# Routed steps of retention plus mixture-of-depths: spread over slots, compared from PSUM, two routing banks

## The chip, the cores and the metric

The kernel runs on one core of one Trainium2 chip. A core has TensorE (PE, matrix products into PSUM), VectorE (DVE), ScalarE (ACT), GpSimd (POOL) and the DMA queues, here issued from SyncE (SP) and POOL. Each engine works its own instructions in the order in which the program issues them; between engines there are only semaphores. The metric is device microseconds of one launch; lower is better. The trace is of one profiled execution, and times in it count from the first instruction.

## The reference

Two stages. The first is a recurrent retention over 4 batches, 8 heads, 768 positions and head size 64; the second routes 128 of the 768 tokens of each batch through a small feed-forward network (FFN) and adds the result to them.

```python
# retention, per batch b and head h
state = gamma[h] * state + outer(k[t], v[t])
y[t] = q[t] @ state / sqrt(64)

# mixture of depths; x is y with the heads side by side, 512 wide
scores = x @ w_gate
top = the 128 tokens of each batch with the largest scores
h = relu(x[top] @ w1)              # 512 -> 1024
out = x
out[top] = x[top] + sigmoid(scores[top]) * (h @ w2)
```

## The kernel before

**Retention in chunks.** The decay is folded into q and v by two tables of powers, so that a chunk of 128 positions needs only a masked product of q and k, a product with the running state, and an update of that state. There are 6 chunks to a batch and 24 in all. They come two at a time: block `m` (12 of them) holds chunks 2m and 2m+1, and is loaded, cast and turned as a whole.

**The main loop** goes over the blocks. In block `m` it issues: `load(m + 5)` on SP's queue (3 loads of 512 KB); `cast(m + 3)` on POOL (L147 to L150: q times its table, k, v times its table, to bf16); and then, for each of the block's two chunks, `transposes(m + 2, "q")` or `(..., "k")` (eight PE transposes into `pt`, one ACT copy), `scores(m + 1, ...)` (16 matmuls into `pa`, then DVE multiplies by the mask, L180), `combine` (`py`: the state's part L193, the masked part L199), `update` (state product L214 into `pst`, two ACT copies L219), `finish` (L227: ACT copies `py` to `xo`; L229: DVE multiplies `py` by `w_gate` and sums each row to a gate score), and `put` (store of `xo` on SP's queue).

**Routing.** After a batch's sixth chunk, `routed(b)` gives a list of twelve steps. The main loop takes one step off the list at four places in each block, before `combine` and after `finish` of each chunk, so the list lasts three blocks; the last batch's list runs after the loop. The steps are:

- `route_rows` (two steps): PE spreads each chunk's 128 scores over all partitions (L249), ACT copies them to `row` (L251).
- `route_beats`: for each of 6 chunks DVE compares the scores pairwise, within the chunk (L260; `before` breaks ties) and against all later chunks (L262, which also counts).
- `route_ranks`: 21 PE matmuls with a column of ones count who beats each token (L271); DVE adds to `rank`, and six compares with `slot` (L280) give one-hot rows `P`.
- `route_index`: 12 matmuls turn `P` into token numbers; DVE casts them to `idx` (L293).
- `route_fetch`: POOL issues a gather of 128 rows of the output (L299). One step is empty after it.
- `route_turn` and `route_gate`: PE turns the rows, ACT copies them (`xT`); DVE multiplies by `w_gate` and sums (L319), ACT and DVE make the sigmoid.
- `ffn_up` twice (16 matmuls each, L335, and an ACT relu into `hT`), `ffn_down` (8 matmuls, L343, and DVE's scaled add into `ye`, L345), `route_put` (POOL issues the scatter, L350).

**Order and buffers.** The schedule is manual: instructions stand on each engine in the order of these calls. PSUM is split by pools: `psT` 2 banks for `pt`, `psA` the two-bank `pa`, `psY` 2 for `py`, `psS` 1 for `pst`, `psM` 1 for everything of the routing. Two engines that read the same PSUM tile are ordered by a semaphore: L229 waits for L227. Loads have 5 buffers each and `xo` has 4. Since SP's queue is in order, `load(m + 5)` stands behind the stores of block m - 1; on POOL the gather and the scatter stand between the casts.

Of the kernel before, what the change touches and what calls it, by code (L numbers as in the profile page):

```python
# [18 lines left out]
def kernel(ctx: ExitStack, tc: tile.TileContext, q, k, v, w_gate, w1, w2, capacity, out):  # L19
    nc = tc.nc  # L20
# [24 lines left out]
    psT = ctx.enter_context(tc.tile_pool(name="psT", bufs=2, space=bass.MemoryType.PSUM))  # L45
# [3 lines left out]
    psM = ctx.enter_context(tc.tile_pool(name="psM", bufs=1, space=bass.MemoryType.PSUM))  # L49
# [56 lines left out]
    slot = consts.tile([128, C], BF)  # L106
    before = consts.tile([128, C], FT)
    tok = consts.tile([128, 1 + NBC], BF)
    above = consts.tile([128, NC], FT)

    def route_tables():
        slot_i = consts.tile([128, C], I32)
        nc.gpsimd.iota(slot_i, pattern=[[1, C]], base=0, channel_multiplier=0)
        nc.vector.tensor_copy(slot, slot_i)
        nc.gpsimd.memset(before, TINY)
# [6 lines left out]
        above_i = consts.tile([128, NC], I32)  # L122
        nc.gpsimd.iota(above_i, pattern=[[-C, NC]], base=C * (NC - 1), channel_multiplier=0)
        nc.vector.tensor_copy(above, above_i)
# [115 lines left out]
    def route_rows(b, lo):  # L240
        st = batch[b]
        if lo == 0:
            st["row"] = perb.tile([128, S], FT, name="row", tag="row")
            st["beats"] = perb.tile([128, NC, S], BF, name="beats", tag="beats")
            st["lost"] = perb.tile([128, NC], FT, name="lost", tag="lost")
        n = min(4, NC - lo)
        pr = psM.tile([128, n * C], FT, name="pr", tag="pm")
        for j in range(n):
            nc.tensor.transpose(pr[:, j * C:(j + 1) * C],  # L249
                                st["sc"][:, lo + j:lo + j + 1].to_broadcast([128, C]), identf)  # L250
        nc.scalar.activation(st["row"][:, lo * C:(lo + n) * C], pr, AF.Copy)  # L251


    def route_beats(b, blocks):
        st = batch[b]
        row, g = st["row"], st["beats"]
        for I in blocks:
            s = st["sc"][:, I:I + 1]
            lo, hi = I * C, (I + 1) * C
            nc.vector.scalar_tensor_tensor(g[:, I, lo:hi], row[:, lo:hi], s, before, OP.subtract, OP.is_lt)  # L260
            if hi < S:
                nc.vector.tensor_scalar(g[:, I, hi:], row[:, hi:], s, None, OP.is_le, OP.add,  # L262
                                        accum_out=st["lost"][:, I:I + 1])

    def route_ranks(b):
        st = batch[b]
        g = st["beats"]
        pk = psM.tile([128, 512], FT, name="pk", tag="pm")
        for J in range(NC):
            for I in range(J + 1):  # L270
                nc.tensor.matmul(pk[:, J:J + 1], g[:, I, J * C:(J + 1) * C], ones,  # L271
                                 start=(I == 0 and J == 0), stop=True, skip_group_check=True)
        won = perb.tile([128, NC], FT, name="won", tag="won")
        nc.vector.tensor_sub(won[:, :NC - 1], above[:, :NC - 1], st["lost"][:, :NC - 1])
        nc.vector.tensor_copy(won[:, NC - 1:], above[:, NC - 1:])
        rank = perb.tile([128, NC], FT, name="rank", tag="rank")
        nc.vector.tensor_add(rank, pk[:, :NC], won)
        P = perb.tile([128, NC, C], BF, name="P", tag="P")
        for J in range(NC):
            nc.vector.tensor_scalar(P[:, J, :], slot, rank[:, J:J + 1], None, OP.is_equal)  # L280
        st["P"] = P

    def route_index(b):
# [8 lines left out]
        idx = perb.tile([128, 1], I32, name="idx", tag="idx")  # L292
        nc.vector.tensor_copy(idx, pi[:, 0:1])  # L293
        st["idx"] = idx

    def route_fetch(b):
        st = batch[b]
        xg = perb.tile([128, Dm], FT, name="xg", tag="xg")
# [16 lines left out]
    def route_gate(b):  # L315
        st = batch[b]
        junk = store.tile([C, H, D], BF, name="junk", tag="junk")
        ssel = perb.tile([128, 1], FT, name="ssel", tag="ssel")
        nc.vector.scalar_tensor_tensor(junk.opt(), st["xg"], 1.0, wgB, OP.mult, OP.mult, accum_out=ssel)  # L319
# [19 lines left out]
    def ffn_down(b):  # L339
        st = batch[b]  # L340
        pd = psM.tile([128, Dm], FT, name="pd", tag="pm")
        for ff in range(FB):
            nc.tensor.matmul(pd, st["hT"][:, ff, :], w2s[:, ff, :], start=(ff == 0), stop=(ff == FB - 1))  # L343
        ye = perb.tile([128, Dm], FT, name="ye", tag="ye")
        nc.vector.scalar_tensor_tensor(ye, pd, st["gate"][:, 0:1], st["xg"], OP.mult, OP.add)  # L345
        st["ye"] = ye
# [7 lines left out]
    def routed(b):  # L354
        return [
            lambda: route_rows(b, 0),
            lambda: (route_rows(b, 4), route_beats(b, range(0, 2))),
            lambda: route_beats(b, range(2, NC)),
            lambda: route_ranks(b),
            lambda: route_index(b),  # L360
            lambda: route_fetch(b),
            lambda: None,
            lambda: (route_turn(b), route_gate(b)),
            lambda: ffn_up(b, 0),
            lambda: ffn_up(b, 1),
            lambda: ffn_down(b),
            lambda: route_put(b),
        ]


# [11 lines left out]
    pending = []  # L382

    def step():
        if pending:
# [67 lines left out]
```

## Time and profile before

| what | value |
|---|---|
| median of 3 runs | 178.52 us (177.93 to 178.78) |
| the profiled execution, its own time | 179.37 us |
| its span, first to last instruction | 177.5 us |
| mean granted TensorE clock | 0.831 |
| busy: PE, DVE, ACT, POOL | 119.0, 84.0, 69.9, 72.7 us |
| first attention product of block 0 | at 22.65 us |
| HBM read and written | 24.38 MB, 7.34 MB |

The page cuts the span in 40 slices of 4.44 us and gives each engine's busy share in tenths, the clock that TensorE was granted, and the share of the DMA engines. A group's line gives line number, engine, operation, output and inputs, shapes and count; then busy time and the mean of one in ns; then how long the engine sat idle just before them and what ended that. A line of the timeline gives start, duration, engine, source line, operation and, in brackets, the idle time before it and its releaser. A matmul row can merge several matmuls. Loads of weights into PE are counted apart (PEld) and lie beside the matmuls.

### The profile page before, as it was taken

The numbers are of one execution on the slowest core, as the hardware profiler recorded it, in microseconds if no ns is written. First come the engines' busy times: TensorE is split into PE (matmuls) and PEld (weight loads), VectorE is DVE, ScalarE is ACT, GpSimd is POOL, SyncE is SP. The second block draws the span as 40 slices with busy tenths as digits, with TensorE's granted clock in tenths as the row PEclk, the third lists the DMA queues.
The fourth block names the chain that finished last, engine by engine and source line by source line (L and its number), as shares of the span: only waits on it lengthen the run. The fifth ranks groups of instructions, "written<-read, shape, count | busy, mean of one in ns | idle before, by whom it ended". The sixth has DMA issues, their size and how long they took to land. (4 is left out here: it accounts for less than half of the span.)

```text
span 177.5 us, 3719 instructions
## 1 busy us (share of the span) xinstructions
PE 119.0 (67%) x1528; PEld 92.6 (52%) x1532; DVE 84.0 (47%) x204; ACT 69.9 (39%) x129; POOL 72.7 (41%) x64
## 2 busy tenths in 40 slices
PE   0325299658969279699931499999479798342860
PEld 0314178546758158586820388868258684132720
DVE  1032045343074993544589954655993512851010
ACT  8135076442365324456760036668503452201110
POOL 7898970268966906600796039002002001120002
PEclk9999999999999999999995555699855558955567
DMA  4999999999999999696495003113303201301001
GB/s 136 297 299 290 275 216 213 252 298 285 340 315 322 326 312 310 205 278 198 118 301 174 4 0 122 59 63 118 120 2 93 90 0 59 118 0 59 4 0 59
DMA packets 43265, 29.86 MB, mean 168 GB/s; under 512 B 1136, under 2 KB 39024, under 8 KB 43248
## 3 DMA queue, kind: packets, MB, share of 16 engines
q1 hardware_dynamic: 41040, 25.43, 51.7%
q0 software_dynamic: 2208, 4.19, 10.4%
q8 instruction: 12, 0.20, 0.4%
q14 instruction: 5, 0.04, 0.1%
HBM read 24.38 MB, written 7.34 MB: 179 GB/s over the span
## 5 line engine op out<-in xcount | busy, mean ns | idle before, releaser
L229 DVE SCALAR_TENSOR_TENSOR junk<-py,wgB 128x512 bf16<-128x512 f32 x24 | 16.5, 689 | 46.6 <-ACT xo L227 46.6
L180 DVE TENSOR_TENSOR am<-pa,causal 128x1024 bf16<-128x1024 f32 x24 | 29.3, 1219 | 12.5 <-PE pa L177 12.3
L162 ACT ACTIVATE qT<-pt 128x1024 bf16<-128x1024 bf16 x12 | 15.8, 1319 | 32.2 <-PE pt L159 32.2
L219 ACT ACTIVATE S<-pst 64x256 bf16<-64x256 f32 x40 | 15.1, 378 | 33.3 <-PE pst L214 32.8
L150 POOL TENSOR_TENSOR vb<-vf,gv 128x1024 bf16<-128x1024 f32 x12 | 22.8, 1900 | 6.1 <-DMA vf<-in_v_dram 6.1
L350 POOL DMA_INDIRECT out_dram<-ye,idx x4 | 4.1, 1037 | 50.4 <-DVE ye L345 38.9
L147 POOL TENSOR_TENSOR qb<-qf,gq 128x1024 bf16<-128x1024 f32 x12 | 22.8, 1904 | 2.6 <-DMA qf<-in_q_dram 2.3
L159 PE MATMUL pt<-ident,qb 128*128 128x128 bf16 x96 | 11.6, 296 | 17.6 <-POOL qb L147 17.6
L271 PE MATMUL pk<-ones,beats 128*128 128x1 bf16 x84 | 8.9, 175 | 18.9 <-DVE beats L260 11.5
L199 PE MATMUL py<-vb,am 64*128 64x64 bf16 x384 | 21.5, 222 | 0.0
L199 PEld LDWEIGHTS <-am 64*128 64x128 bf16 x384 | 18.1, 115 | 4.2 <-issue 3.6
L159 PEld LDWEIGHTS <-qb 128*128 128x128 bf16 x96 | 9.0, 136 | 18.8 <-POOL qb L147 18.3
L299 POOL DMA_INDIRECT xg<-out_dram,idx x4 | 4.3, 1074 | 34.3 <-DVE idx L293 34.3
L227 ACT ACTIVATE xo<-py 128x512 f32<-128x512 f32 x24 | 14.3, 597 | 9.9 <-PE py L199 7.1
L214 PE MATMUL pst<-vb,kb 64*128 64x128 bf16 x160 | 18.2, 281 | 0.0
L271 PEld LDWEIGHTS <-beats 128*128 128x128 bf16 x84 | 5.5, 105 | 22.7 <-DVE beats L260 15.0
L260 DVE SCALAR_TENSOR_TENSOR beats<-row,sc,before 128x128 bf16<-128x128 f32 x24 | 17.0, 710 | 0.0
L177 PE MATMUL pa<-qT,kT 64*64 64x128 bf16 x384 | 14.1, 289 | 3.0 <-DVE am L180 1.7
L149 POOL CAST kb<-kf 128x1024 bf16<-128x1024 f32 x12 | 12.5, 1042 | 7.2 <-DMA kf<-in_k_dram 7.2
L335 PE MATMUL ph<-xT,w1s 128*128 128x128 bf16 x128 | 13.4, 289 | 2.4 <-ACT xT L311 1.7
L214 PEld LDWEIGHTS <-kb 64*128 64x128 bf16 x160 | 14.3, 128 | 0.0
L335 PEld LDWEIGHTS <-w1s 128*128 128x128 bf16 x128 | 11.9, 135 | 3.8 <-issue 3.6
(62 smaller groups left out, 151.9 us busy)
## 6 DMA issues: line engine op xcount, KB each, us to landing
qf<-in_q_dram SPq DMA_DIRECT2D x12, 512.0 KB, 6.3
kf<-in_k_dram SPq DMA_DIRECT2D x12, 512.0 KB, 7.4
vf<-in_v_dram SPq DMA_DIRECT2D x12, 512.0 KB, 7.6
out_dram<-xo SPq DMA_DIRECT2D x24, 256.0 KB, 3.8
w1s<-in_moe_w_dram POOLq DMA_DIRECT2D x1, 1024.0 KB, 10.9
w2s<-in_moe_w_dram POOLq DMA_DIRECT2D x1, 1024.0 KB, 17.2
wgB<-in_moe_w_gate_dram SPq DMA_DIRECT2D x1, 256.0 KB, 6.3
xg<-out_dram,idx POOLq DMA_INDIRECT x4, 3.4
```

The costliest lines, as they stand in the source:

```text
L147: nc.gpsimd.tensor_mul(qb, raw["q", m].rearrange("p h j d -> p j h d"), gq[:, 2 * r:2 * r + 2, :, None].to_broadcast([128, 2, H, D]))
L150: nc.gpsimd.tensor_mul(vb, raw["v", m].rearrange("p h j d -> p j h d"), gv[:, 2 * r:2 * r + 2, :, None].to_broadcast([128, 2, H, D]))
L159: nc.tensor.transpose(pt[:, j, dd, :], src[:, j, 2 * dd:2 * dd + 2, :], ident)
L162: nc.scalar.activation(t.rearrange("p h (s j) -> p j h s", j=2), pt, AF.Copy)
L180: nc.vector.tensor_mul(am.rearrange("p a b c d -> p (a b c d)"), pa.rearrange("p a b c d -> p (a b c d)"), causal.rearrange("p a b c -> p ...
L199: nc.tensor.matmul(py[:, h, :], att[m, dd // 2][r, half, dd % 2, j, :], vb[r, j, h, :], start=(c == 0 and h == 0 and j == 0), stop=True, s ...
L214: nc.tensor.matmul(pstate[b][:, dd, :], kb[r, j, 2 * dd:2 * dd + 2, :], vb[r, j, 2 * dd:2 * dd + 2, :], start=(c == 0 and dd == 0 and j == ...
L219: nc.scalar.activation(t[r, :, half * 64:half * 64 + 64], pstate[b][r, :, half * 64:half * 64 + 64], AF.Copy)
L229: nc.vector.scalar_tensor_tensor(junk.opt(), py.opt(), 1.0, wgB, OP.mult, OP.mult, accum_out=batch[b]["sc"][:, c:c + 1])
L260: nc.vector.scalar_tensor_tensor(g[:, I, lo:hi], row[:, lo:hi], s, before, OP.subtract, OP.is_lt)
L271: nc.tensor.matmul(pk[:, J:J + 1], g[:, I, J * C:(J + 1) * C], ones, start=(I == 0 and J == 0), stop=True, skip_group_check=True)
L335: nc.tensor.matmul(ph[:, j, :], w1s[:, dd, ff * 128:(ff + 1) * 128], st["xT"][:, dd, :], start=(j == 0 and dd == 0), stop=True, skip_group ...
```

## The change

**Slots.** The list of steps is replaced by a table of slots. Chunk i begins at slot t = 2i; slot t is worked between `scores` and `combine`, slot t + 1 between `finish` and `put`; what is left after the loop is worked in order. `route_spread` of a chunk is at t + 3 and `route_beats` at t + 4, so that each chunk of a batch is compared while later ones are still being computed, with the earlier chunks of its batch in place of the later ones. After a batch's last chunk follow ranks (t + 5), hot rows (t + 6), index (t + 7), fetch (t + 8), turn and gate (t + 11), sigmoid and the first `ffn_up` (t + 12), the second (t + 13), `ffn_down` (t + 14), `ffn_add` (t + 15), put (t + 16). For batch 2 the slots t + 12 and t + 13 fall in chunk 23, the rest after the loop.

**Engines and operands.** The comparison within the chunk reads the spread scores `pr` in PSUM; ACT's copy of `pr` to `row` is issued behind it (the program gives it a semaphore wait on that comparison). The counts of the first five chunks are made by `route_part`, after the fifth, so that `route_ranks` has six matmuls left, and one that spreads the slot numbers over the partitions of PSUM. One compare of 768 columns makes `P`, with the slot numbers read from PSUM. The gate product moves from DVE to a POOL multiply (L335 of the new file) and an ACT copy with a sum (L337). Several steps are cut where they change engine, so that the DVE part falls in a later slot than the PE part.

**Banks.** `psT` has one bank in place of two, `psM` two in place of one.

```diff
-    psT = ctx.enter_context(tc.tile_pool(name="psT", bufs=2, space=bass.MemoryType.PSUM))
+    psT = ctx.enter_context(tc.tile_pool(name="psT", bufs=1, space=bass.MemoryType.PSUM))
...
-    psM = ctx.enter_context(tc.tile_pool(name="psM", bufs=1, space=bass.MemoryType.PSUM))
+    psM = ctx.enter_context(tc.tile_pool(name="psM", bufs=2, space=bass.MemoryType.PSUM))
...
-    slot = consts.tile([128, C], BF)
+    slot = consts.tile([1, C], BF)
+    one = consts.tile([1, C], BF)
...
-    above = consts.tile([128, NC], FT)
+    won = consts.tile([128, NC], FT)
...
+    def route_spread(b, c):
+        st = batch[b]
+        if c == 0:
+            st["row"] = perb.tile([128, S - C], FT, name="row", tag="row")
             st["beats"] = perb.tile([128, NC, S], BF, name="beats", tag="beats")
+            st["part"] = perb.tile([128, NC], FT, name="part", tag="part")
+        pr = psM.tile([128, C], FT, name="pr", tag="pm")
+        nc.tensor.transpose(pr, st["sc"][:, c:c + 1].to_broadcast([128, C]), identf)
+        st["pr"] = pr
+
+    def route_beats(b, c):
+        st = batch[b]
+        row, g, pr = st["row"], st["beats"], st["pr"]
+        lo, hi = c * C, (c + 1) * C
+        s = st["sc"][:, c:c + 1]
+        nc.vector.scalar_tensor_tensor(g[:, c, lo:hi], pr, s, before, OP.subtract, OP.is_lt)
+        if c < NC - 1:
+            nc.scalar.activation(row[:, lo:hi], pr, AF.Copy)
+        if c:
+            acc = won[:, c:c + 1] if c < NC - 1 else st["part"][:, c:c + 1]
+            nc.vector.tensor_scalar(g[:, c, :lo], row[:, :lo], s, float(lo), OP.is_lt, OP.subtract, accum_out=acc)
+
+    def route_part(b):
...
         pk = psM.tile([128, 512], FT, name="pk", tag="pm")
+        for J in range(NC - 1):
+            for c in range(J, NC - 1):
+                nc.tensor.matmul(pk[:, J:J + 1], g[:, c, J * C:(J + 1) * C], ones,
+                                 start=(J == 0 and c == 0), stop=True, skip_group_check=True)
+        st["pk0"] = pk
+
+    def route_part_add(b):
+        st = batch[b]
+        nc.vector.tensor_add(st["part"][:, :NC - 1], st["pk0"][:, :NC - 1], won[:, :NC - 1])
+
+    def route_ranks(b):
...
+        nc.tensor.matmul(pk[:, C:2 * C], one, slot, start=True, stop=True, skip_group_check=True)
         for J in range(NC):
...
+            nc.tensor.matmul(pk[:, J:J + 1], g[:, NC - 1, J * C:(J + 1) * C], ones,
+                             start=False, stop=True, skip_group_check=True)
+        st["pk"] = pk
+
+    def route_hot(b):
...
+        nc.vector.tensor_add(rank, pk[:, :NC], st["part"])
         P = perb.tile([128, NC, C], BF, name="P", tag="P")
-        for J in range(NC):
-            nc.vector.tensor_scalar(P[:, J, :], slot, rank[:, J:J + 1], None, OP.is_equal)
+        nc.vector.tensor_tensor(P, pk[:, None, C:2 * C].to_broadcast([128, NC, C]),
+                                rank[:, :, None].to_broadcast([128, NC, C]), OP.is_equal)
...
     def route_gate(b):
         st = batch[b]
-        junk = store.tile([C, H, D], BF, name="junk", tag="junk")
+        prod = perb.tile([128, Dm], FT, name="prod", tag="prod")
+        nc.gpsimd.tensor_mul(prod, st["xg"], wgB)
         ssel = perb.tile([128, 1], FT, name="ssel", tag="ssel")
-        nc.vector.scalar_tensor_tensor(junk.opt(), st["xg"], 1.0, wgB, OP.mult, OP.mult, accum_out=ssel)
+        nc.scalar.activation(prod, prod, AF.Copy, accum_out=ssel)
...
+    for i in range(NBC):
+        b, c = divmod(i, NC)
+        t = 2 * i
+        at(t + 3, route_spread, b, c)
+        at(t + 4, route_beats, b, c)
+        if c == NC - 2:
+            at(t + 5, route_part, b)
+            at(t + 6, route_part_add, b)
+        if c == NC - 1:
+            for d, f in ((5, route_ranks), (6, route_hot), (7, route_index), (8, route_fetch), (11, route_turn),
+                         (11, route_gate), (12, route_sigmoid)):
+                at(t + d, f, b)
+            at(t + 12, ffn_up, b, 0)
+            at(t + 13, ffn_up, b, 1)
+            at(t + 14, ffn_down, b)
+            at(t + 15, ffn_add, b)
+            at(t + 16, route_put, b)
...
+        for u, nm in enumerate(("q", "k")):
+            t = 2 * (2 * m + u)
+            if m + 2 < NBLK:
+                transposes(m + 2, nm)
+            if m + 1 < NBLK:
+                scores(m + 1, u)
+            slot_work(t)
+            py = combine(m, u)
+            update(m, u)
+            xo = finish(m, u, py)
+            slot_work(t + 1)
+            put(m, u, xo)
+    for t in sorted(slots):
+        slot_work(t)
```

## The prediction

> **What bounds the kernel now.** I read the page first, then the groups with their shapes, the timeline around the longest waits, the stretches with the clock, and the end of the timeline. The chain of waits breaks off at the last gather, so the timeline had to carry the rest.
>
> The page (slices of 4.44 us):
>
> ```profile
> span 177.5 us, 3719 instructions
> PE 119.0 (67%) x1528; PEld 92.6 (52%) x1532; DVE 84.0 (47%) x204; ACT 69.9 (39%) x129; POOL 72.7 (41%) x64
> ...
> PE   0325299658969279699931499999479798342860
> ...
> POOL 7898970268966906600796039002002001120002
> PEclk9999999999999999999995555699855558955567
> DMA  4999999999999999696495003113303201301001
> ```
>
> No engine is full over the span. DMA is full for about 72 us, then nearly idle; PE is full in most slices after that, with holes near 60, 93, 127 and 155 us. Until about 50 us PE waits for data. Two groups (columns: busy us, mean ns; idle before):
>
> ```profile
> L271 PE MATMUL pk<-ones,beats 128*128 128x1 bf16 x84 | 8.9, 175 | 18.9 <-DVE beats L260 11.5 <-DVE beats L262 5.0 <-ACT row L251 0.5
> L260 DVE SCALAR_TENSOR_TENSOR beats<-row,sc,before 128x128 bf16<-128x128 f32 x24 | 17.0, 710 | 0.0
> ```
>
> PE idles 18.9 us ahead of the rank counts. The comparison has a median of 344 ns but a mean of 710: three of the 24 took 1.94, 1.56 and 6.33 us. The timeline shows what lay beside the longest:
>
> ```profile
> 89.48 1.89 POOL L150 TENSOR_TENSOR vb<-vf,gv 128x1024 bf16<-128x1024 f32 x1
> ...
> 89.89 6.33 DVE L260 SCALAR_TENSOR_TENSOR beats<-row,sc,before 128x128 bf16<-128x128 f32 x1
> ...
> 94.18 1.89 POOL L150 TENSOR_TENSOR vb<-vf,gv 128x1024 bf16<-128x1024 f32 x1
> 96.14 0.87 DVE L262 TENSOR_SCALAR_CACHE_REDUCE beats<-row,sc 128x640 bf16<-128x640 f32 x1
> ...
> 96.28 0.18 PE L271 MATMUL pk<-ones,beats 128*128 128x1 bf16 x1 [6.03 <-DVE beats L260]
> ```
>
> The comparison starts under a POOL multiply and ends when POOL's unbroken run of five ends (94.18 + 1.89 = 96.07). The other two also end with a POOL multiply. Comparisons with two SBUF tensors (`row`, `before`) are held; the counting form (L262, one tensor) never was. Excess: 17.0 - 24 x 0.344 = 8.7 us. The holes also cost clock (columns of interest: PE busy, then after POOL the granted clock):
>
> ```profile
> 84.00:88.00 4.00, 4.00 (x78) 3.17 (x76) 2.59 (x4) 2.48 (x4) 2.44 (x2) 1.00 0.29 98
> 104.00:108.00 4.00, 4.00 (x55) 3.14 (x53) 1.13 (x3) 1.87 (x4) 3.06 (x3) 0.50 0.22 66
> 120.00:124.00 4.00, 4.00 (x86) 3.21 (x82) 1.93 (x4) 3.57 (x7) 1.04 (x1) 1.00 0.35 131
> ```
>
> At 0.50 the eight transposes of a half block take 1.04 us, at 1.00 0.61. (Before about 79 us the column says 1.00 while they take 1.04; I read that stretch as slow.) The clock rises near 79, 113 and 148 us, each time during `ffn_up` or `ffn_down`, and falls after each hole.
>
> The end:
>
> ```profile
> 149.49 0.64 PE L199 MATMUL py<-vb,am 64*128 64x64 bf16 x16
> ...
> 158.75 1.03 POOL L299 DMA_INDIRECT xg<-out_dram,idx  x1 [7.33 <-DVE idx L293]
> ...
> 173.51 1.01 POOL L350 DMA_INDIRECT out_dram<-ye,idx  x1 [13.72 <-DVE ye L345]
> ```
>
> The last attention product (I count 24 chunks, 0 to 23) ends at 150.1; 8.65 us later the last gather is issued, and 18.75 us after that the span ends. The profiled execution took 179.37 us, 1.87 over its span and 0.85 over the median 178.52.
>
> **The change part by part.**
>
> *To chunk 6's state copy* (54.1 us before): data-bound. The added spreads and comparisons hide under that. One PSUM bank for turned q and k makes each turn wait for the previous copy (1.3 us), but turns are 4 us apart. I take 54.4.
>
> *Comparisons.* All 24 now take `pr` from PSUM, so one SBUF tensor. The 8.7 us go and 24 x 0.344 stays. Could PSUM be dearer? L229 reads `py` from PSUM in 691 ns; L319, the same operation on SBUF, takes 689: nothing. The Trainium skill ("Perfetto Trace Analysis", Optimizing Scalar/DVE Operations) gives DVE about 60 ns of overhead on SBUF and 125 on PSUM; by it 24 x 65 ns = 1.6 us more. The row is the same shape on this chip, so I keep nothing.
>
> *A new wait.* `row`'s copy on ACT now waits for the comparison that reads the same bank, as L229 waits for L227's copy of `py` today (46.6 us of DVE waiting). Behind it on ACT stand the state copy and `xo`. This closes a ring: state copy 0.80, `xo` 0.63, gate score 0.62, mask product 1.14 (1.22 less overlap), comparison 0.40, `row` 0.25 (128x256 takes 0.379, 128x512 0.588, so 0.27), next state copy. That is 3.85 us a chunk, in which PE has about 2.4 us of attention at the high clock (87.94 to 90.2: 2.3, plus one spread 0.15) and 4.2 at the low one (24.47 to 28.36: 3.9, plus 0.26). So attention is PE-bound at the low clock and ring-bound at the high one.
>
> *Chunks 6 to 12, low clock.* Six chunks x 4.2 = 25.2. Batch 0's routed work on the way: seven rank matmuls 0.8 (13 in 1.5), hot rows on DVE 1.1, index 0.64, turn 0.9, two halves of `ffn_up` 1.7 and 1.4, `ffn_down` 1.8: 8.3. Less 1.5 for state products that chunks 11 and 12 don't have. 54.4 + 32.0 = 86.4, against 87.8 before.
>
> *Chunks 12 to 23.* Nothing now holds DVE for 6 us, and PE has work in every chunk, so I expect the clock up from `ffn_up` (about 80) on. Eleven rings x 3.85 = 42.4. Extra per batch: `ye` 0.75 and, as a spread needs the bank that `ye` frees, turn and scores behind it 1.1; hot rows 1.15 (six compares take 1.07; the 768-wide form scaled from L180 0.91, at most 1.22); `idx` and gate 0.5; the FFN's ACT copies 1.5: 5.0, twice. Less 2 for the last four chunks, which have no turns and then no scores. 50.4. The last product stands 1.8 ahead of that point: 86.4 + 48.6 = 135.0. At the low clock throughout, PE needs 11 x (4.2 + 1.8 of routed work) = 66, and the product ends at about 150.6. I take three quarters high: 135.0 + 0.25 x 15.6 = 138.9.
>
> *Gate product.* Moved from DVE (0.69) to POOL: 1.90/2 = 0.95, at most 1.9, plus an ACT sum near 0.6 (`xo` 0.597). POOL's queue puts the casts of one block (4.85) between gather and product, ACT waits up to 1.5 us once a batch (inside my 5.0). At the end it runs beside turn, copy and `ffn_up`: `e` is due 2.8 us after the rows land, the first `hT` at 3.8, so nothing.
>
> *The end.* Batch 2's second `ffn_up` and `ffn_down` move behind chunk 23's product, ahead of the last spread. From the product: `ffn_up` 1.0, `hT` 0.75, `ffn_down` 1.8, fifteen counts 1.5 (they hide `ye`, the scatter's wait), spread 0.2, two compares 1.35, counts 0.8, hot rows 1.3, index 0.8, `idx` and issue 0.5: 10.0 instead of 8.65. Low clock throughout would make it 12.5. Gather to end stays 18.75.
>
> Sum: 138.9 + 10.0 + 18.75 = 167.7 of span, plus 1.87: 169.5 beside 179.37, which is 9.9 less; from the median, 168.6. I state 168.5.
>
> **The rivals.**
>
> 1. *PE stays at the low clock.* For: PE idles about a third of each ring, and the first 79 us show dense attention without a rise. Against: from 84 to 90 and 119 to 125 us attention alone held 1.00, and it fell only after holes of 2.5 to 4 us. Span 150.6 + 12 + 18.75 = 181.4, so 182.3 at the pessimistic end; with the first FFN stretch high, 174. Together: 173 to 182. The skill ("TensorE: Matmul & The Clock Gate", A second HAM failure mode: psum-queue depth-cycling) says frequent short PE idles between groups can make the clock oscillate, which speaks against one turning bank; the whole low clock is what it would make of the time at worst. The two stretches at 1.00 are dense ones, so no row here excludes it.
>
> 2. *The ring is longer than the sum of its rows* (the other side). Place: ACT's copy of `row` behind DVE, once a chunk. The span equals today's if the product ends at 148.75: (148.75 - 54.4)/17 = 5.55 us a chunk, against 4.97 in my sum. Another 0.6 a chunk, for example the counting comparison (0.33 to 0.87) falling inside, turns it to slower; 1 us more gives 186. For: six handovers, each across engines, on in-order queues. Against: the durations include today's handovers.
>
> 3. *The ring doesn't bind*: ACT is often late anyway and PE, all high, sets 3.45 a chunk: product at 127, time about 157.
>
> 4. *The stalls go but were slack.* Before, DVE's 6.3 us left PE idle for 6.03, so I give this little: 178.
>
> **How the numbers follow.** Forecast (160 to 173) 0.60; rival 1 0.16, of which 0.05 above 179.4; rival 2 0.12; rival 3 (below 160) 0.08; rival 4 0.04. Half a per cent is 0.9 us, about what three runs from 177.93 to 178.78 can tell. Faster: 0.60 + 0.10 + 0.08 = 0.78 with most of rival 1; same: 0.05; slower: 0.17. The range reaches into rivals 1 and 2 above and rival 3 below: 159 to 181.
>
> **What would show it.** All 24 comparisons near 0.35 us; DVE's wait on `xo` still long; a new ACT wait of `row` on the comparison of about 0.5 us, some twenty times; no PE hole over 3 us between 55 and 135 us; the clock at 1.00 from about 80 to the last gather; the last gather near 149. I am wrong if the clock column shows 0.50 for most of 90 to 135, if state copies stand over 5 us apart where no FFN runs, or if POOL multiplies still lengthen a DVE comparison.

## The result and the profile after

| | before | predicted | after |
|---|---|---|---|
| median, us | 178.65 (177.93 to 179.05, 4 runs) | 168.5 | 166.8 (165.17 to 168.52, 4 runs) |
| ratio to before, 95% interval | | | 0.9311 [0.9231, 0.939] |
| state copy of chunk 6 starts | 54.12 | 54.4 | 53.90 |
| state copy of chunk 12 starts | 87.84 | 86.4 | 84.91 |
| last attention product ends | 150.1 | 138.9 | 139.73 |
| last gather issued | 158.75 | 148.9 | 149.14 |
| span ends | 177.5 | 167.7 | 164.7 |

The kernel is 11.9 us faster. The ratio leaves out the run of 168.52, which is over 1.5% above the fastest of its kernel. The profiled execution took 166.44 us, 1.74 over its span. The page of the kernel after, in slices of 4.12 us:

```profile
span 164.7 us, 3709 instructions
PE 117.8 (72%) x1532; PEld 92.9 (56%) x1536; DVE 72.6 (44%) x173; ACT 74.9 (45%) x149; POOL 77.7 (47%) x67
...
PE   0234289984969799968976899999489868830770
...
POOL 7978993039895682588606706900200220022302
PEclk9999999999999999999998555569955555985589
```

The empty stretch of PE that stood near 93 us before is gone, and DVE is busy 72.6 us where it was busy 84.0. But the clock row is not the forecast one: from slice 23 (about 91 us) it says 5 more often than 9. Three groups (busy us, mean ns; idle before, and what ended it):

```profile
L258 DVE SCALAR_TENSOR_TENSOR beats<-pr,sc,before 128x128 bf16<-128x128 f32 x24 | 8.2, 342 | 0.5 <-PE pr L250 0.5
...
L260 ACT ACTIVATE row<-pr 128x128 f32<-128x128 f32 x20 | 5.5, 276 | 20.7 <-DVE beats L258 20.7
...
L250 PE MATMUL pr<-identf,sc 128*128 128x128 f32 x24 | 10.1, 421 | 7.0 <-DVE ye L372 5.4 <-DVE junk L229 1.4
```

The first: 24 comparisons cost 8.2 us of DVE, not 17.0, and the longest is 0.351. The second is the forecast wait of the row copy, twice as long as forecast. The third was not priced as a stop of PE: the spread needs a routing bank that `ye` (L372, the add that ends the FFN) still reads. The timeline of the kernel after shows the first such wait:

```profile
84.80 0.53 PE L271 MATMUL pk<-ones,beats 128*128 128x1 bf16 x15
...
86.34 0.69 DVE L229 SCALAR_TENSOR_TENSOR junk<-py,wgB 128x512 bf16<-128x512 f32 x1 [2.12 <-ACT xo L227]
...
86.95 0.75 DVE L372 SCALAR_TENSOR_TENSOR ye<-pd,gt,xg 128x512 f32<-128x512 f32 x1
...
87.76 0.32 PE L250 MATMUL pr<-identf,sc 128*128 128x128 f32 x1 [2.43 <-DVE ye L372]
```

The last matmul of `ye`'s input ends at 83.85, but `ye` stands on DVE behind the gate score of the next chunk, which waits for ACT's copy. PE stands for 2.43 us, again for 2.43 at 118.30, and for 0.49 in the tail. The stretches with the clock (length; busy and instructions of PE, PEld, DVE, ACT, POOL; clock; DMA share; GB/s):

```profile
84.00:88.00 4.00, 1.57 (x41) 1.37 (x38) 1.58 (x5) 1.35 (x3) 0.01 (x1) 1.00 1.16 310
...
100.00:104.00 4.00, 4.00 (x54) 3.18 (x52) 1.97 (x8) 2.84 (x5) 3.63 (x3) 0.50 0.36 117
...
116.00:120.00 4.00, 1.70 (x40) 1.39 (x41) 1.46 (x4) 1.72 (x3) 1.04 (x1) 1.00 0.17 66
```

Both waits fall where the clock is at 1.00, and it drops within 1.8 us of the end of each (89.4 and 120.1). The end of the span, after and then before:

```profile
138.70 1.03 PE L199 MATMUL py<-vb,am 64*128 64x64 bf16 x16
...
149.14 1.04 POOL L316 DMA_INDIRECT xg<-out_dram,idx  x1 [3.31 <-DVE idx L313]
...
154.39 3.47 PE L358 MATMUL ph<-xT,w1s 128*128 128x128 bf16 x32 [0.69 <-ACT xT L328]
...
157.70 1.89 PE L366 MATMUL pd<-w2s,hT 128*128 128x512 bf16 x7
...
160.66 1.04 POOL L377 DMA_INDIRECT out_dram<-ye,idx  x1 [6.77 <-DVE ye L372]
```

```profile
164.07 1.86 PE L335 MATMUL ph<-xT,w1s 128*128 128x128 bf16 x16 [0.68 <-ACT xT L311]
...
166.62 1.87 PE L335 MATMUL ph<-xT,w1s 128*128 128x128 bf16 x16 [0.68 <-ACT hT L337]
...
169.98 2.46 PE L343 MATMUL pd<-w2s,hT 128*128 128x512 bf16 x6 [0.22 <-issue]
```

With one routing bank the second half of `ffn_up` waited for the relu `hT` of the first, and `ffn_down` waited again and ran at the low clock. With two banks the halves run as one row, the clock rises at 157.6, and `ffn_down` takes 1.89; before it rose only at 172.0, near the end of `ffn_down`, which took 3.27 (169.17 to 172.44). From the start of `ffn_up` to the end of `ffn_down` it is 159.59 - 154.39 = 5.20 against 172.44 - 164.07 = 8.37 (169.98 + 2.46 ends at 172.44). Of the 3.17 us saved, 1.37 are the two waits of PE for `hT` (0.69 and 0.68); most of the rest is the clock. That the clock rises sooner because the row has no gaps is read from these rows. No run isolates it, but the same stretch takes 8.61 us in the first experiment below, which has one bank, and 3.67 to 5.61 in the other nine, which have two (3.67 where the clock was up already).

### The profile page after: what moved, and what is told of

Same layout as the page of the kernel before. It is cut to its first block, busy times and chain, and to the rows that moved or that the text cites. A ratio compares the mean times of both kernels' runs of the same rounds, so it can differ in the third digit from the quotient of the medians.

```text
span 164.7 us, 3709 instructions
## 1 busy us (share of the span) xinstructions
PE 117.8 (72%) x1532; PEld 92.9 (56%) x1536; DVE 72.6 (44%) x173; ACT 74.9 (45%) x149; POOL 77.7 (47%) x67
## 3 DMA queue, kind: packets, MB, share of 16 engines
q0 software_dynamic: 2208, 4.19, 11.1%
## 4 chain that ended last, share of the span: by engine, by line
PE 31%; DMA 23%; DVE 13%; SPq 12%; issue 11%; ACT 5%; POOL 1%; POOLq 1%
DMA qf<-in_q_dram 11%; SPq L62 11%; DMA xg<-out_dram,idx 9%; PE ph L358 5%; PE pt L159 5%; DVE am L180 5%; PE pa L177 4%; PE py L199 4%; DMA out_dram<-xo 3%; PE pd L366 3%; PE pr L250 2%; ACT xo L227 2%; PE pst L214 2%; DVE beats L263 2%; PE pg L326 2%
## 5 line engine op out<-in xcount | busy, mean ns | idle before, releaser
L180 DVE TENSOR_TENSOR am<-pa,causal 128x1024 bf16<-128x1024 f32 x24 | 29.4, 1223 | 21.0 <-PE pa L177 20.7
L199 PE MATMUL py<-vb,am 64*128 64x64 bf16 x384 | 22.7, 228 | 0.0
L199 PEld LDWEIGHTS <-am 64*128 64x128 bf16 x384 | 19.1, 119 | 4.7 <-issue 4.3
L219 ACT ACTIVATE S<-pst 64x256 bf16<-64x256 f32 x40 | 15.0, 376 | 13.7 <-PE pst L214 13.2
L214 PE MATMUL pst<-vb,kb 64*128 64x128 bf16 x160 | 19.9, 299 | 0.0
L159 PEld LDWEIGHTS <-qb 128*128 128x128 bf16 x96 | 10.1, 142 | 16.3 <-POOL qb L147 15.9
L165 ACT ACTIVATE kT<-pt 128x1024 bf16<-128x1024 bf16 x12 | 12.2, 1020 | 8.1 <-PE pt L159 7.9
L214 PEld LDWEIGHTS <-kb 64*128 64x128 bf16 x160 | 15.7, 138 | 0.0
L250 PE MATMUL pr<-identf,sc 128*128 128x128 f32 x24 | 10.1, 421 | 7.0 <-DVE ye L372 5.4
L260 ACT ACTIVATE row<-pr 128x128 f32<-128x128 f32 x20 | 5.5, 276 | 20.7 <-DVE beats L258 20.7
L159 PE MATMUL pt<-ident,kb 128*128 128x128 bf16 x96 | 11.7, 296 | 2.9 <-ACT qT L162 2.2
L358 PE MATMUL ph<-xT,w1s 128*128 128x128 bf16 x128 | 12.6, 281 | 1.2 <-ACT xT L328 1.2
## 6 DMA issues: line engine op xcount, KB each, us to landing
w2s<-in_moe_w_dram POOLq DMA_DIRECT2D x1, 1024.0 KB, 17.1
```

Of the source, the lines that this page charges most:

```text
L159: nc.tensor.transpose(pt[:, j, dd, :], src[:, j, 2 * dd:2 * dd + 2, :], ident)
L180: nc.vector.tensor_mul(am.rearrange("p a b c d -> p (a b c d)"), pa.rearrange("p a b c d -> p (a b c d)"), causal.rearrange("p a b c -> p ...
L199: nc.tensor.matmul(py[:, h, :], att[m, dd // 2][r, half, dd % 2, j, :], vb[r, j, h, :], start=(c == 0 and h == 0 and j == 0), stop=True, s ...
L214: nc.tensor.matmul(pstate[b][:, dd, :], kb[r, j, 2 * dd:2 * dd + 2, :], vb[r, j, 2 * dd:2 * dd + 2, :], start=(c == 0 and dd == 0 and j == ...
L358: nc.tensor.matmul(ph[:, j, :], w1s[:, dd, ff * 128:(ff + 1) * 128], st["xT"][:, dd, :], start=(j == 0 and dd == 0), stop=True, skip_group ...
```

## The experiments

All ratios are to the kernel before, on the same chip (medians 178.65 to 178.7).

### One SBUF tensor in the old comparison

The kernel before, with the comparison inside a chunk as the counting form, so without the table `before` (and what it decides, the order of equal scores).

```diff
+st["spare"] = perb.tile([128, NC], FT, name="spare", tag="spare")
...
-nc.vector.scalar_tensor_tensor(g[:, I, lo:hi], row[:, lo:hi], s, before, OP.subtract, OP.is_lt)
+nc.vector.tensor_scalar(g[:, I, lo:hi], row[:, lo:hi], s, None, OP.is_lt, OP.add,
+                        accum_out=st["spare"][:, I:I + 1])
```

> The kernel before with one edit: the comparison within a chunk becomes the counting form with one SBUF tensor (row below the token's score), as L262 already is; ties between tokens are no longer broken by position. Theory (DVE held under POOL's multiplies, 8.7 us, and PE idle behind it): all 24 comparisons at 0.33 to 0.36 us plus 0.08 for the sum; the 6.0 us hole of PE at 90 to 96 goes, the clock stays at 1.00 longer, span 8 to 13 us shorter, 166 to 171 us. Rival (the gain comes from spreading the routed work, the stalls were slack): 177 to 179 us.

Measured: 169.68 us (169.33 to 170.53), ratio 0.9495 [0.945, 0.954]. The group in this kernel:

```profile
L261 DVE TENSOR_SCALAR_CACHE_REDUCE beats<-row,sc 128x128 bf16<-128x128 f32 x24 | 8.2, 342 | 0.0
```

Nothing else of the program was changed, and 9.0 us went: the stalls were no slack. The masked product that ended at 105.13 before ends about 7 us earlier.

### The other half: slots and banks, with two SBUF tensors

The kernel after, with the row copied first (now for all six chunks of a batch) and the comparison reading row and table from SBUF.

```diff
-st["row"] = perb.tile([128, S - C], FT, name="row", tag="row")
+st["row"] = perb.tile([128, S], FT, name="row", tag="row")
...
-nc.vector.scalar_tensor_tensor(g[:, c, lo:hi], pr, s, before, OP.subtract, OP.is_lt)
-if c < NC - 1:
-    nc.scalar.activation(row[:, lo:hi], pr, AF.Copy)
+nc.scalar.activation(row[:, lo:hi], pr, AF.Copy)
+nc.vector.scalar_tensor_tensor(g[:, c, lo:hi], row[:, lo:hi], s, before, OP.subtract, OP.is_lt)
```

> The changed kernel with the comparison reading row (after ACT's copy) and the table, both in SBUF, as before the change; slots, banks and the rest stay. Theory (held under POOL): of the 24 comparisons those that meet a POOL multiply take 1 to 6 us, 5 to 10 us in all, and the time rises by 2 to 8 us to 169 to 175 us, since the slots give DVE some slack. Rival (the slots alone make the gain, a long comparison is now hidden): within 1 us of 166.8. Second rival (the wait of row's copy on the comparison cost more): faster than 166.

Measured: 169.8 us (169.52 to 171.05), ratio 0.9508 [0.9458, 0.9558]. Its group, and its timeline around the longest comparison:

```profile
L259 DVE SCALAR_TENSOR_TENSOR beats<-row,sc,before 128x128 bf16<-128x128 f32 x24 | 20.4, 850 | 4.7 <-ACT row L258 4.7
```

```profile
90.67 3.44 DVE L259 SCALAR_TENSOR_TENSOR beats<-row,sc,before 128x128 bf16<-128x128 f32 x1
91.06 1.04 POOL L149 CAST kb<-kf 128x1024 bf16<-128x1024 f32 x1
92.06 1.89 POOL L150 TENSOR_TENSOR vb<-vf,gv 128x1024 bf16<-128x1024 f32 x1
...
94.97 0.32 PE L284 MATMUL pk<-ones,beats 128*128 128x1 bf16 x6 [3.47 <-DVE beats L262]
```

The comparison is held again until POOL's last multiply ends (92.06 + 1.89 = 93.95, against 90.67 + 3.44 = 94.11). The excess is even larger than in the kernel before, 20.4 - 24 x 0.342 = 12.2 us against 8.7, but it costs only 3.0 us of time beside the kernel after, and 4.2 beside the next version (165.58), which differs from this one only in the operand and the copy of the sixth chunk's row. My reading, not shown by a run: in the slots most comparisons have later work of PE beside them, and only some are followed at once by rank counts. So the two halves of the change overlap: the stalls alone are worth 9.0, the rest alone 8.9, both together 11.9. Of the 8.9, 3.1 fall behind the last gather, which this version issues 15.65 us before its end; slots and banks were not taken apart further.

### Row copy ahead of the comparison

```diff
-nc.vector.scalar_tensor_tensor(g[:, c, lo:hi], pr, s, before, OP.subtract, OP.is_lt)
 if c < NC - 1:
     nc.scalar.activation(row[:, lo:hi], pr, AF.Copy)
+nc.vector.scalar_tensor_tensor(g[:, c, lo:hi], pr, s, before, OP.subtract, OP.is_lt)
```

> The changed kernel with row's copy issued ahead of the comparison, so that DVE waits for ACT and not ACT for DVE; both still read the spread scores in PSUM. Ring theory (ACT's copy of row behind DVE holds the state copy): ACT's 20.7 us of waiting for the comparison goes; state copies start up to 0.6 us earlier in a few chunks at the low clock, more at the high one; 1 to 3 us faster, 164 to 166 us. Rival (PE sets the pace at the low clock, the ring has slack): within 0.7 us of 166.8.

Measured: 165.58 us (164.89 to 166.83), ratio 0.9267 [0.9213, 0.932], beside 0.9311 [0.9231, 0.939] of the kernel after. The two groups of this kernel:

```profile
L260 DVE SCALAR_TENSOR_TENSOR beats<-pr,sc,before 128x128 bf16<-128x128 f32 x24 | 8.3, 344 | 4.8 <-ACT row L259 4.4 <-PE pr L250 0.3
L259 ACT ACTIVATE row<-pr 128x128 f32<-128x128 f32 x20 | 5.4, 269 | 0.3 <-PE pr L250 0.3
```

ACT's 20.7 us of waiting are gone; DVE waits 4.4 us for the row instead; the time moves by 1.2 us, within what the intervals allow as nothing. ACT's wait was mostly cover: the state copies then wait 32.7 us for PE's state product, where they waited 13.2. A run at the end takes this up again.

### `ye` one slot earlier

`ffn_add` in the slot of `ffn_down`, issued behind that slot's comparisons.

```diff
-            at(t + 15, ffn_add, b)
+            late.append((t + 14, ffn_add, b))
...
+    for t, f, b in late:
+        at(t, f, b)
```

> The changed kernel with the scaled add ye one slot earlier, behind the comparisons of that slot and ahead of the chunk's gate score, so that the bank is free when the next spread wants it. Theory (PE's 2.43 us wait for ye costs its own length and the clock): both waits go, 4 to 5 us, the clock stays at 1.00 beyond 89 and 120 us, and the chunks behind gain up to 1 us each; 156 to 163 us. Rival (the wait alone, the clock falls anyway): 161 to 163 us. Rival (another wait takes its place): 165 to 167 us.

Measured: 160.35 us (159.43 to 162.76), ratio 0.8949 [0.89, 0.8998], 6.4 us below the kernel after. Its group, and PE around the place where the wait was:

```profile
L250 PE MATMUL pr<-identf,sc 128*128 128x128 f32 x24 | 9.9, 412 | 2.1 <-DVE junk L229 1.3 <-DVE ye L372 0.5
```

```profile
87.88 0.23 PE L283 MATMUL pk<-slot,one 1*128 1x128 bf16 x1 [0.67 <-DVE part L277]
...
88.93 0.30 PE L285 MATMUL pk<-ones,beats 128*128 128x1 bf16 x6 [0.82 <-DVE beats L263]
```

The wait for `ye` falls from 5.4 to 0.5 us. The clock still drops at 89.3 and at 116.6 (10.2 us after its rise, as in the kernel after), and PE now stands 0.67 and 0.82 us for the sum of the earlier counts and for the last comparison. So the gain is mostly the wait's own length, 4.9 us, and it does not come through longer high stretches. The other 1.5 us were not traced.

### PE kept busy in the wait

Fourteen matmuls of 384 columns into unused columns of the bank, behind the partial counts, in the kernel after.

```diff
+        for _ in range(14):
+            nc.tensor.matmul(pk[:, 128:512], ident, w1s[:, 0, 0:384], start=True, stop=True, skip_group_check=True)
         st["pk0"] = pk
```

> The changed kernel with fourteen extra matmuls of 384 columns into unused columns of the counts' bank, issued where PE waits for ye (2.43 us); their results are read by nobody. Theory (the clock falls at 89.4 and 120.1 us because PE idles in the stretch before, and the low clock is worth time): the fall comes at least 3.4 us later in both places, the wait itself stays covered, and the time drops by 1 to 4 us, 163 to 166 us. Rival (the wait costs only its length, attention is bound by DVE and ACT at either clock): within 0.8 us of 166.8. Rival (the clock doesn't follow PE's idling): falls stay where they are, and the fillers add up to 1 us.

Measured: 166.72 us (165.9 to 167.54), ratio 0.9345 [0.9298, 0.9391]: the time of the kernel after. The filler fills the wait (2.44 us of it at 88.11), and the clock does stay: the drop moves from 89.4 to 100.2 and from 120.1 to 124.0. (The means, 0.844 and 0.876, say little: ahead of the first rise the column counts as 1.00, though the transposes take 1.04 there.) The stretches of this kernel:

```profile
92.00:96.00 4.00, 3.12 (x71) 2.44 (x69) 3.33 (x8) 2.66 (x5) 3.97 (x3) 1.00 0.37 138
96.00:100.00 4.00, 2.84 (x69) 2.27 (x65) 2.34 (x5) 2.35 (x6) 0.76 (x1) 1.00 0.04 14
```

So the drop depends on what PE does in the stretch ahead of it. The filler changes two things there, the idle time and the kind of product (128x128 weights, 384 columns), and the run doesn't separate them. The longer high clock does help: chunks 14, 15 and 20 take 3.72, 4.24 and 3.35 us from product to product, where the kernel after takes 5.33, 4.87 and 4.60 at the low clock, 3.5 us less. In batch 0, where PE had no such wait, the filler did something that was not expected:

```profile
55.21 4.38 PE L274 MATMUL pk<-w1s,ident 128*128 128x384 bf16 x14
...
59.54 0.61 PE L159 MATMUL pt<-ident,kb 128*128 128x128 bf16 x8
...
77.00 1.11 PE L328 MATMUL pg<-identf,xg 128*128 128x128 f32 x4 [3.98 <-DMA xg<-out_dram,idx]
```

The clock rose at 59.2, right behind it, and stayed at 1.00 until 76.3, through attention and the small products of the routing; the kernel after is at the low clock there (its transposes take 1.06). Chunks 8, 9 and 10 took 3.72, 4.08 and 3.38 us instead of 4.57, 4.87 and 4.19, some 0.8 less each. But the filler's own 4.38 us made batch 0's gather 3.0 us later (70.62 against 67.66), PE then waited 3.98 us for the rows instead of 2.24, the clock fell at 76.3, and the first half of `ffn_up` ran at the low one. So chunk 11's product comes 2.85 us late (82.97 against 80.12). The filler also takes 2.44 us between the last product and the gather. The last product comes 1.04 us earlier, the gather at 149.26 instead of 149.14. As an isolation of the clock's worth the run is not clean; it shows 0.6 to 1.6 us for a plain chunk.

### Gate product back on DVE

```diff
-        prod = perb.tile([128, Dm], FT, name="prod", tag="prod")
-        nc.gpsimd.tensor_mul(prod, st["xg"], wgB)
+        junk = store.tile([C, H, D], BF, name="junk", tag="junk")
         ssel = perb.tile([128, 1], FT, name="ssel", tag="ssel")
-        nc.scalar.activation(prod, prod, AF.Copy, accum_out=ssel)
+        nc.vector.scalar_tensor_tensor(junk.opt(), st["xg"], 1.0, wgB, OP.mult, OP.mult, accum_out=ssel)
```

> The changed kernel with the gate product back on DVE, one instruction with a sum, both inputs in SBUF, as before the change; the slots stay. Theory (POOL's product is off the path, DVE has slack): within 0.8 us of 166.8. Rival (held under POOL's casts as the comparisons were): the two products that meet casts take 2 to 6 us and the time rises by 1 to 4 us. Rival (POOL and ACT were late with it): ACT's queue is free earlier, 1 us faster.

Measured: 165.54 us (164.97 to 165.92), ratio 0.9276 [0.9236, 0.9316]. The group of the product, four in all:

```profile
L336 DVE SCALAR_TENSOR_TENSOR junk<-xg,wgB 128x512 bf16<-128x512 f32 x4 | 3.9, 984 | 4.0 <-DMA xg<-out_dram,idx 4.0
```

One of the four was held on DVE: it took 1.87 us at 75.39, beside a multiply and a cast of POOL, the other three 0.69 as in the kernel before. In time the intervals overlap; no gain of the move to POOL shows, and it cost perhaps 1.3 us.

### FFN of batch 2 behind the last gather

The kernel after, with batch 2's second `ffn_up`, `ffn_down`, `ye` and scatter put behind batch 3's gather.

```diff
+            if b == B - 2:
+                for d, f, more in ((21, ffn_up, (1,)), (21, ffn_down, ()), (22, ffn_add, ()), (24, route_put, ())):
+                    at(t + d, f, b, *more)
+                continue
```

> The changed kernel with batch 2's second ffn_up, ffn_down, ye and scatter issued behind the last gather in place of ahead of the last spread. Theory (in the end stage these 1.4 + 0.8 + 1.9 us stand on the path to the last gather, and PE idles 4.5 us while it lands): the last gather is issued about 3 us earlier, 163 to 164.5 us, less if the scatter then holds up POOL. Rival (the last scores, not PE, set when the last spread can start): within 1 us of 166.8.

Measured: 163.8 us (162.41 to 164.79), ratio 0.9176 [0.9108, 0.9243]. The gather is issued at 147.66, 1.5 us earlier, half of what was expected. In this version the clock fell at 116.2 and stayed at 0.50 until 150.3, where the kernel after had 1.00 from 140.6 to 147.4. The span ends 13.7 us after the gather instead of 15.6: batch 2's FFN runs while the rows are fetched, the clock is up when they land, and the last `ffn_up` takes 1.95 us where it took 3.47.

### Three waits of PE at once

The kernel after with the row copy first, `ye` early, and the ranks one slot later, in the slot of the hot rows:

```diff
-            for d, f in ((5, route_ranks), (6, route_hot),
+            for d, f in ((6, route_ranks), (6, route_hot),
```

> The changed kernel with three edits: row's copy ahead of the comparison, ye in the slot of ffn_down, and the last rank counts one slot later, behind the next chunk's scores, so that PE doesn't wait for DVE's last comparison (0.7 and 0.77 us in the changed kernel, 0.82 and 0.67 us with the early ye). Theory (PE's short idles in one clock window of 3.4 us let the clock fall, and the ring binds at the high clock): the clock stays at 1.00 for 4 windows or more after each FFN instead of 3, and the time is 3 to 8 us below the early ye alone (160.4): 152 to 157 us. Rival (each edit gives its own wait back and no more): 157.5 to 159.5 us.

Measured: 157.43 us; its runs lie between 154.57 and 158.32, too far apart for a ratio. The last product ends at 131.69, the gather is issued at 140.77. The median lies at the border of the two forecasts and doesn't decide between them. Of the clock, half came as the theory said: behind batch 0's FFN it stays at 1.00 for 13.65 us (four times 3.41) where the kernel after has 10.24, behind batch 1's it falls 10.2 us after its rise at 104.5, as in the kernel after. Up to chunk 14's product PE still stops once at the high clock, for 0.76 us: the next spread needs the bank that `part`, the sum of the earlier counts, still reads. What sets the pace of chunk 14 here is DVE. Its timeline, with that stop of PE:

```profile
86.88 0.34 DVE L260 SCALAR_TENSOR_TENSOR beats<-pr,sc,before 128x128 bf16<-128x128 f32 x1
87.11 0.29 PE L250 MATMUL pr<-identf,sc 128*128 128x128 f32 x1 [0.76 <-DVE part L277]
87.13 0.87 DVE L263 TENSOR_SCALAR_CACHE_REDUCE beats<-row,sc 128x640 bf16<-128x640 f32 x1
...
87.93 0.69 DVE L229 SCALAR_TENSOR_TENSOR junk<-py,wgB 128x512 bf16<-128x512 f32 x1
...
88.54 1.22 DVE L180 TENSOR_TENSOR am<-pa,causal 128x1024 bf16<-128x1024 f32 x1
...
89.87 0.96 DVE L295 TENSOR_TENSOR P<-pk,rank 128x768 bf16<-128x768 f32 x1
```

No row of DVE has idle time in brackets. The products of chunks 13 and 14 end 3.51 us apart, with DVE full for that time.

### All four edits, and the ring once more

The three edits above and batch 2's FFN behind the gather:

> The kernel after, with four edits at once: the row copy ahead of the comparison, the add of the routed sum one slot earlier behind the comparisons, the ranks one slot later, and batch 2's second ffn_up, its ffn_down, add and scatter behind the last gather. Theory 'each edit gives back its own wait': the three waits together stood at 157.4 and the move of the tail was worth 3.0 alone (166.8 to 163.8), so 154 to 155.5. Rival 'the tail's move paid only because the last stretch of attention was late': 156.5 to 158, since the last product now comes at 130.7 instead of 139.7. Last gather expected 1.5 us before the 140.8 of the run with three waits.

The same three edits without the row copy first (`ye` early, ranks later):

> The kernel after with the add one slot earlier and the ranks one slot later, but the comparison still ahead of the row copy: what the wait of ACT for the comparison costs once TensorE's waits of 2.43 are gone. Theory 'the ring through row copy and comparison binds as soon as nothing else stops TensorE' (the prediction's): 3 to 5 us more than the 157.4 with the row copy first, so 160.5 to 162.5. Rival 'ring is slack, the row copy first is worth what it was alone, 0.4 to 1.2 us': 157.5 to 159. The wait of ACT for the comparison should be back at about 20 us in sixteen to twenty parts in both.

Measured on one chip: all four 153.37 us (152.17 to 153.76), ratio 0.8584 [0.8492, 0.8675], the fastest version here, a little below the 154 to 155.5 of the theory. Without the row copy first and without the moved FFN 158.39 us (156.72 to 160.23), ratio 0.8824 [0.8704, 0.8944], in the range of the rival, beside the 157.43 with the row copy first. By the medians the row copy first is thus worth 1.0 us, which the spread of both (3.5 and 3.8 us) can't tell from nothing or from 3; ACT's wait for the comparison is back at 20.8 us. The rows say more: at the full clock (up to the last product of chunk 20) chunks 14 and 20 take 3.51 and 3.68 us in it, and 3.51 and 3.73 with the row copy first, so the order of copy and comparison doesn't set their pace. The moved FFN adds 4.1 us by the medians (157.43 - 153.37), which the same spread doesn't tell from the 3.0 it gave alone; its gather comes at 138.22 and the end 13.8 us later. The end of the kernel with all four:

```profile
138.22 1.05 POOL L316 DMA_INDIRECT xg<-out_dram,idx  x1 [10.97 <-DVE idx L313]
...
138.76 3.31 PE L366 MATMUL pd<-w2s,hT 128*128 128x512 bf16 x8
...
143.19 1.95 PE L358 MATMUL ph<-xT,w1s 128*128 128x128 bf16 x32 [0.69 <-ACT xT L328]
...
144.97 1.89 PE L366 MATMUL pd<-w2s,hT 128*128 128x512 bf16 x8
```

The first `ffn_down` runs in the shadow of the gather, at the low clock (3.31); the second, on the path, at the full one (1.89).

Going back to two banks for `psT` and one for `psM` was not tried: with one routing bank this order of slots cannot run (a spread would wait for the hot rows, which DVE has behind a mask product of scores that PE has behind the spread). What the second bank is worth by itself is read from the tail's rows only.

## Why the prediction was right, and where it wasn't

The forecast was 168.5 us and the measurement 166.8, inside the likeliest case. The mechanism of the comparisons was right; the total owes much to luck. By its own steps:

- *To chunk 6's state copy*: 54.4 forecast, 53.90 measured. The one bank for turned q and k made PE wait 2.2 us in all, in two waits within the first 30 us, where data set the pace. *Chunks 6 to 12*: 32.0 forecast, 31.0 measured.
- *Comparisons*: right, mechanism and size. Undoing the operand alone brings the stalls back, and removing the second SBUF tensor alone from the kernel before removes them. The 8.7 us of DVE were worth 9.0 us there, and undoing the operand costs 3.0 to 4.2 within the new order. One reading was off: while the longest comparison was held, four operations of POOL ran, not five (the whole run had six). The free PSUM operand is confirmed: 342 ns from PSUM after, a median of 344 for the same operation from SBUF before. The Trainium skill ("Perfetto Trace Analysis", Optimizing Scalar/DVE Operations) sets about 60 ns of overhead on SBUF and 125 on PSUM against that; the 65 ns between them do not show in these rows.
- *A new wait*: ACT waits as said, but 20.7 us in 16 waits instead of some 10 in twenty, and it hardly counts. The pace at the high clock, 3.5 to 3.7 us for chunks 14 and 20 once PE's long waits are gone, is near the 3.85 of the ring, but for another reason: DVE's own work fills it. The ring through the row copy isn't what binds there, since the order of copy and comparison made no difference to these chunks.
- *Chunks 12 to 23*, the clock: wrong. The step took the clock as "three quarters high". It was high for 4.44 + 10.24 = 14.68 of the 54.8 us between chunk 12's copy and the last product, 27%. By the same working the last product would stand at 135.0 + 0.73 x 15.6 = 146.4; it came at 139.73 from a start 1.5 us earlier, so the stretch itself is 5.2 us shorter than that. Two faults in the price of the low clock account for most of it (worked out from rows, not shown by a run). The all-low figure, 11 x (4.2 + 1.8), lacked the deduction for the last chunks, which have no turns: chunks 20 to 22 took 4.60, 4.01 and 3.45 us where chunks 14 to 16 took 5.33, 4.87 and 4.19, 2.3 less. And the share was spread evenly, 15.6/11 = 1.4 us a chunk, while the clock rises in `ffn_up`, so that chunk 18 had it with the second `ffn_up` (1.07 instead of 1.87), `ffn_down` (1.90 instead of 3.31) and some 1.2 us of attention (0.28, 0.61, 0.42 and 0.64 instead of 0.42, 1.06, 0.64 and 1.03), about 3.4 us in all or 2.0 over its share. The 0.9 left I did not trace.
- In the same step, `ye` and what stands behind it were priced at 1.85 us a batch. The two waits took 2.43 each, and taking them away gave 6.4: the place was named, but not that it stops PE where the clock is high.
- *Gate product*: 1.26 us on POOL, above the 0.95 taken and below the 1.9; off the path, as said, within about 1 us.
- *The end*: product to gather 9.4 against 10.0. "Gather to end stays 18.75" failed: 15.6. The mis-sized term is the FFN of the last batch, 5.20 instead of 8.37 us, which accounts for the whole 3.15: 1.37 in waits, most of the rest in the clock. The change to two banks was in the diff, and the row with `hT` in its bracket in the trace of before.

So the sum was right through errors that cancel, which is luck. From the forecast span of 167.7 to the 164.7 measured: the clock low for 73% in place of 25%, 0.48 x 15.6 = 7.5 us more; its price too dear, 5.2 less; up to chunk 12, 1.5 less; product to gather, 0.6 less; the tail, 3.2 less.

The rivals. The first (PE stays at the low clock) met most of its condition and not its price: 173 to 182 us assumed that the low clock costs every chunk alike. The passage of the Trainium skill weighed there ("TensorE: Matmul & The Clock Gate", A second HAM failure mode: psum-queue depth-cycling) has short idles between groups make the clock oscillate, and here it did go up and down, with waits of 0.7 to 2.4 us in the stretches ahead of the drops; that the idle time alone is the cause is not shown. The second (a longer ring) did not occur: no state or row copy of the ring set the pace in any stretch that I read. The third (no ring, 157) is near what the kernel takes once PE's waits are shortened, 157.43, but by accident: the rival had PE all high, and there the clock is still low for most of the time between chunk 12 and the last product. The fourth (slack stalls) is refuted by the first experiment.

Of what should have shown: comparisons near 0.35, no hole of PE over 3 us (the longest is 2.43) and the gather near 149 held; the clock at 1.00 from 80 us on did not, and the sign named for being wrong, 0.50 for most of 90 to 135 us, came up while the time stayed right. A second such sign came up too: state copies over 5 us apart where no FFN runs (84.91, 90.91 and 96.67). It meant a longer ring, but what lies between the first two is PE's wait for `ye`, and between the last two the low clock.

## What to carry to other kernels

Price a clock state chunk by chunk and not as an average: a rise that comes with the FFN falls on work that halves with it (1.87 to 1.07 and 3.31 to 1.90 us here), while a full clock over chunks that DVE holds to 3.5 us gives back much less. A bank that the next slot needs must be released by its reader in the slot before; one DVE add issued behind a waiting gate score cost 6.4 us here. And when a change adds a bank, go through the waits of the tail too, since a wait there counted in full.

## What the runs showed of the hardware

**The clock moves in steps of 3.41 us.** The high stretches last 10.24 us (three times 3.41) twice and then 6.83 (twice) in the kernel after, 13.65 (four times) at 114 us in the kernel before, 17.1 (five times) with the filler, 3.4 in one place of the version with all four edits. Cut at these borders, the stretches of that version read:

```profile
97.25:100.66 3.41, 3.41 (x35) 3.15 (x35) 1.71 (x5) 1.92 (x6) 3.41 (x3) 0.50 0.20 77
100.66:104.07 3.41, 3.41 (x44) 2.85 (x42) 2.22 (x5) 2.58 (x6) 0.61 (x1) 0.50 0.20 77
104.07:107.48 3.41, 3.41 (x62) 2.66 (x63) 2.42 (x6) 2.76 (x6) 0.00 (x0) 1.00 0.22 82
...
110.89:114.30 3.41, 2.48 (x56) 1.85 (x54) 3.41 (x8) 2.39 (x5) 0.00 (x0) 1.00 0.43 156
114.30:117.71 3.41, 2.96 (x52) 2.41 (x53) 2.56 (x6) 1.31 (x4) 0.00 (x0) 0.50 0.21 79
```

A stretch in which PE was busy for 2.48 of 3.41 us was followed by the low clock. In the twelve traces, cut in this way from the first rise of an FFN to the last gather, the stretches ahead of a drop have 0.17 to 2.53 us of PE, those that kept the clock 2.37 to 3.41, so busy time alone does not quite decide. Behind the last gather, where PE has little but FFN products, less sufficed: 1.92 us in the kernel after (157.62 to 161.03), 1.53 with the gate product on DVE. The Trainium skill ("TensorE: Matmul & The Clock Gate", What's actually happening) gives a free-running window of 3413 ns, which agrees, and speaks of a return to the low clock after an idle window; here a window that was 73% busy sufficed.

**Busy is not enough for a rise.** PE was busy for the whole of 97.25 to 100.66 us, with attention and the turn of the fetched rows, and the clock stayed at 0.50; in this version it rose at 104.07, after the stretch in which `ffn_up` starts (101.74). It need not be the FFN: with the filler the clock rose at 59.2, behind a stretch (55.78 to 59.19) that held the filler's 128x128x384 products and nothing else, and where the other versions ran attention at the low clock. Once up, it stayed there through four such stretches of attention and small routing products, with 2.55 to 2.88 us of PE in each. Which property of the products counts was not separated.

**A held comparison waited for all of POOL's run** in the longest case of two kernels: 6.33 us through four operations in the kernel before, 3.44 through the rest of three in the version with two SBUF tensors; the same table in SBUF with its other operand in PSUM was never held in any of the 24 (at most 0.351). **A POOL multiply is not proportional to its size**: 128x512 took 1.264 us and 128x1024 took 1.90 (the first writes fp32, the second bf16).
